# A convolution branch re-cut into a table of slots, with the order on three engines held as traced

## The chip, the cores and the metric

The program runs on one core of a Trainium2 chip. The metric is the device time of one execution in microseconds (us). Work is done by TensorE (PE in the profile; its weight loads are PEld), VectorE (DVE), ScalarE (ACT) and GpSimd (POOL). SyncE (SP) and, in the output stage, ScalarE's queue issue the DMA transfers.

## The reference

The function computed is a layer norm followed by two branches that are summed with the input, and then its whole backward pass: the value and the nine gradients are the outputs. B_x is an input that is not used.

```python
def _A_ref(q, k, v, shift_k, ssm_k, ssm_D):      # convolution branch
    k_shift = sum over 4 taps of k shifted by t * shift_k
    kv = k_shift * v
    y = irfft(rfft(kv padded to 2S) * rfft(ssm_k padded to 2S))[:S]
    y = y + kv * ssm_D
    return q * y

def _B_ref(x, W_gate, W_up, W_down):             # MLP branch
    gate = relu(x @ W_gate); up = x @ W_up
    return (gate * up) @ W_down

xn = _layernorm(A_q)
out = A_q + _A_ref(xn, A_k, A_v, A_shift_k, A_ssm_k, A_ssm_D) + _B_ref(xn, B_W_gate, B_W_up, B_W_down)
outputs: out and its gradients for A_q, A_k, A_v, A_shift_k, A_ssm_k, A_ssm_D, W_gate, W_up, W_down, given grad_out
```

The functions are condensed here. S is 2048, D is 1024, F is 3584, and everything is bf16.

## The kernel before

Two generators are interleaved while the program is traced. One, `mlp()` (L1028), yields the steps of the MLP: `hidden` (L699, gate, up and the gradient of the hidden layer, 8 matmuls of 128x512 a step), `grad_down` (L815) and `grad_in` (L850, weight gradients, also 8 matmuls a step). There are 336, 112 and 224 steps, and each yields 1730, meant as ns. In `hidden`, for each block of 512 columns and each pair of row tiles, the steps are two of gate (`ps_g`, relu by ScalarE, L726), two of up (`ps_u`, two VectorE operations, L733 and L735) and two of down (`ps_h`, a ScalarE copy L748 and a VectorE product L749). The first block, called ahead in the code, orders them differently, since it runs beside the layer norm.

The other generator is the convolution branch, `ABranch.steps` (L425). It treats the 1024 channels in 8 groups of 128. The transforms are two-stage DFTs by small matmuls against tables: `fwd1_filter` and `fwd1` (first stage), a transposition on VectorE (`flip`, L304, two operations of 1024 elements each), `fwd2` (second stage), `cmul` (complex products, ten VectorE operations), `inv_a`, `flip` and `inv_b` or `inv_b_chan` (inverse). ScalarE evicts the PSUM of all of them (L70). `taps` is the four-tap shift (seven VectorE operations, L74), `gate_grad` multiplies the gradient by xn, `grad_taps` and `grad_k` make the gradients of the shift, `loads_1` and `loads_2` load a group's data, and `h_tile` transposes the filter.

The main loop (L1033 to L1045) keeps a balance: each MLP step takes its ns times a pace (0.9 in `hidden`, 1.0 after it) from `left`, which begins at 55,000, and whenever `left` is at or under zero, the branch goes on to its next yield, which adds the ns it names. When the branch ends, its pools close and `open_right` (L868) issues the four loads of `wd`, the down weights of the output stage. Then come `out_phase` (L880 to L913), which needs `wd`, the transposed `hT` and three row tiles a step, and `grad_x`.

The traced order isn't the order on the engines. A scheduler places each instruction by its priority [...]. `Pri.now` (L31) gives the next priority in trace order; `Pri.late` (L35) puts it behind all of these, so that the branch's VectorE and ScalarE operations and its stores fill gaps. An instruction given to `keep_in_program_order` stays in its traced place. Before, that holds for a few: the first group's loads (L84), `shift_rows` (L227), the first sums and one product of the layer norm, and loads of the output stage.

Buffers matter too: the branch has two PSUM tiles (`a_ps`) and the MLP four (`b_ps`); `a_ts` has three buffers that kvt, gkv, gv, gks, yt, gk, hT and ghn share, so that a new one waits until the store of an old one has landed; `a_tmp` has two. Once the branch has closed, `wd` and `hT` take the space of its tiles.

Of the kernel before, what the change touches and what calls it, by code (L numbers as in the profile page):

```python
# [21 lines left out]
class Pri:  # L22
# [4 lines left out]
    def __init__(self, tc):  # L27
        self.tc = tc
        self.n = 0

# [12 lines left out]
class ABranch:  # L43
# [20 lines left out]
    def mm(self, out, lhsT, rhs, start=True, stop=True):  # L64
        self.pri.now()
        self.nc.tensor.matmul(out, lhsT=lhsT, rhs=rhs, start=start, stop=stop)  # L66

    def act(self, out, in_):
        self.pri.late()
        self.nc.scalar.copy(out=out, in_=in_)  # L70

    def tt(self, out, in0, in1, op):
        self.pri.late()
        self.nc.vector.tensor_tensor(out=out, in0=in0, in1=in1, op=op)  # L74

    def vcopy(self, out, in_):
        self.pri.late()
        self.nc.vector.tensor_copy(out=out, in_=in_)
# [11 lines left out]
    def open(self):  # L90
# [7 lines left out]
        self.tmp = self.pool("a_tmp", 2, side=R)  # L98
        self.sm = self.pool("a_sm", 2, side=R)
# [146 lines left out]
    def loads_1(self, gi):  # L246
# [5 lines left out]
        xt = self.tmp.tile([P, 16, P], BF16, name="xt", tag="tmp")  # L252
# [24 lines left out]
    def taps(self, st, out, src, offs):  # L277

        skb = st["skb"]
        for n, (i, off) in enumerate(offs):  # L280
            t = out if n == 0 else self.tmp.tile([P, 16, P], BF16, name="tap", tag="tmp")
            self.tt(t[:, 0:16, :], src[:, off:off + 16, :], skb[:, i, :, :].to_broadcast([P, 16, P]), ALU.mult)
            if n > 0:
                self.tt(out[:, 0:16, :], out[:, 0:16, :], t[:, 0:16, :], ALU.add)

    def h_tile(self, st):
# [4 lines left out]
        for r in range(16):  # L291
            self.pri.now()
            self.nc.tensor.transpose(pst[:, r, :], hv[:, r, :], self.identA[:])
# [3 lines left out]
    def flip(self, src):  # L297

        dst = self.big.tile([P, NB1, P], BF16, name="flp", tag="big")
        df = dst[:].rearrange("p k c -> p (k c)").bitcast(F32).rearrange("p (k cp) -> p cp k", cp=64)  # L300
        sf = src.rearrange("p cp r i -> p (cp r i)").bitcast(F32).rearrange("p (cp r) -> p cp r", cp=64)
        for c0 in range(0, 64, 32):
            self.pri.late()
            self.nc.vector.transpose(out=df[:, c0:c0 + 32, :], in_=sf[:, c0:c0 + 32, :])  # L304
        return dst

    def fwd1_filter(self, hT, sD, ns):
        B = self.big.tile([P, 64, NB1, 2], BF16, name="B", tag="big")
        for r0 in range(0, NB1, 8):
# [6 lines left out]
            if r0 == 0:  # L316
                for rows in (slice(0, 32), slice(64, 96)):
                    b0 = B[rows, :, 0, :]
                    self.tt(b0, b0, sD[rows].rearrange("p (cp i) -> p cp i", i=2), ALU.add)
            if r0 == 24:  # L320
                self.flipped = self.flip(B[:])
            yield ns

    def fwd1(self, src, ns):
        B = self.big.tile([P, 64, 2, 16, 2], BF16, name="B", tag="big")
        for r0 in range(0, 16, 8):
# [7 lines left out]
            if r0 == 8:  # L334
                self.flipped = self.flip(B[:].rearrange("p cp u r i -> p cp (u r) i"))
            yield 2 * ns

    def fwd2(self, Bf, F, ns):
        for j0 in range(0, 4, 2):
# [10 lines left out]
            yield 2 * ns  # L350
# [4 lines left out]
    def cmul(self, X, Z, conj, name):  # L355

        Q = self.form(name)
        for hf in range(2):
# [3 lines left out]
            self.tt(t1[:], X[:, g], Z[:, g], ALU.mult)  # L362
            self.tt(t2[:, 0], X[:, g, 0], Z[:, g, 1], ALU.mult)
            self.tt(t2[:, 1], X[:, g, 1], Z[:, g, 0], ALU.mult)
            self.tt(Q[:, g, 0], t1[:, :, 0], t1[:, :, 1], ALU.add if conj else ALU.subtract)
            self.tt(Q[:, g, 1], t2[:, 0], t2[:, 1], ALU.subtract if conj else ALU.add)
        return Q

    def inv_a(self, Q, ns):
        C = self.big.tile([P, 64, 4, 8, 2], BF16, name="C", tag="big")  # L370
        for j0 in range(0, 4, 2):
# [13 lines left out]
            if j0 == 2:  # L385
                self.flipped = self.flip(C[:].rearrange("p cp q m i -> p cp (q m) i"))
            yield 2 * ns

    def inv_b(self, Cf, dst, ns):
# [8 lines left out]
        yield 2 * ns  # L398

    def inv_b_chan(self, Cf, dst, ns):  # L400
        dv = dst[:, 0:16, :].rearrange("p r c -> p (r c)").rearrange("p (n1 n2) -> p n1 n2", n2=NB1)
        for n0 in range(0, NB1, 16):
# [4 lines left out]
            yield ns  # L407

    def grad_taps(self, gi, gks, kp, ns):


        ps = self.ps.tile([P, 2, 512], F32, name="ps6", tag="aps")
        self.mm(ps[:, 1, 0:3 * P], self.NX[:], gks[:, 0:3, :].rearrange("p r c -> p (r c)"))
        self.act(gks[:, 16:19, :].rearrange("p r c -> p (r c)"), ps[:, 1, 0:3 * P])
        pd = ps[:, 0, 0:P].rearrange("p (i c) -> p i c", i=4)
        for r in range(16):
            for b in range(0, P, 32):
                self.mm(pd[b:b + 32], gks[:, r, b:b + 32], kp[:, r:r + 4, b:b + 32], start=(r == 0), stop=(r == 15))
        dg = self.tmp.tile([P, 4, 32], F32, name="dg", tag="tmp")
        self.tt(dg[:], pd, self.ident32[:].to_broadcast([P, 4, 32]), ALU.mult)  # L420
        self.pri.late()
        self.nc.vector.tensor_reduce(out=self.gs_all[:, gi, :], in_=dg[:], axis=AX.X, op=ALU.add)
        yield ns

    def steps(self):  # L425

# [6 lines left out]
        yield 8000  # L433
        hT = self.h_tile(nx)
        for gi in range(self.NG):
            st, nx = nx, None
            cg, kp, vt, gt = st["cg"], st["kp"], st["vt"], st["gt"]
            yield 2000
            yield from self.fwd1_filter(hT, st["sD"], 2000)
            Hf = self.flipped  # L440
            if gi == 0:
                self.gate_grad(st)
            ksh = self.lng.tile([P, 16, P], BF16, name="ksh")
            self.taps(st, ksh, kp, [(3, 0), (2, 1), (1, 2), (0, 3)])
            kvt = self.ttile("kvt")
            self.tt(kvt[:, 0:16, :], ksh[:], vt[:], ALU.mult)
            yield from self.fwd1(gt, 2000)
            Gf = self.flipped
            H = self.form("H")
            yield from self.fwd2(Hf, H, 1700)  # L450
            if gi + 1 < self.NG:
                nx = self.loads_1(gi + 1)
            yield from self.fwd1(kvt, 1800)
            Kf = self.flipped
            G = self.form("G")
            yield from self.fwd2(Gf, G, 1700)
            if nx is not None:
                self.gate_grad(nx)
            GKV = self.cmul(H, G, True, "GKV")
            yield 2000  # L460
            K = self.form("K")
            yield from self.fwd2(Kf, K, 1700)
            Y = self.cmul(H, K, False, "Y")
            yield 12000
            yield from self.inv_a(GKV, 1800)
            Cg = self.flipped
            yield 5000
            yield from self.inv_a(Y, 1800)
            Cy = self.flipped
            GH = self.cmul(K, G, True, "GH")  # L470
            yield 2000
            gkv = self.ttile("gkv")
            yield from self.inv_b(Cg, gkv, 2000)
            gks = self.gradients(st, gkv, ksh)
            yield 6000
            yt = self.ttile("yt")
            yield from self.inv_b(Cy, yt, 2000)
            self.store_time(self.y_d, cg, yt)
            yield from self.grad_taps(gi, gks, kp, 1800)
            self.grad_k(st, gks)  # L480
            if nx is not None:
# [597 lines left out]
```

## Time and profile before

| what | value |
|---|---|
| median of 3 runs | 1955.04 us (1952.65 to 1960.59) |
| profiled execution, own time | 1959.32 us |
| its span | 1957.5 us |
| TensorE busy | 1898.6 us, 97% |
| VectorE busy | 904.3 us, 46% |
| ScalarE busy | 630.7 us, 32% |
| granted TensorE clock, mean | 0.994 |
| DMA | 319.08 MB, mean 163 GB/s |

The profile is of one execution. A busy time is the sum over an engine's instructions, and idle time is given with what ended it: "[3.72 <-DVE ru L733]" behind an instruction means that its engine stood 3.72 us and that the VectorE instruction of line 733 ended this. Idle time on an engine other than the one that sets the end costs nothing by itself. In the windows the columns are the window and its length, busy us and number of instructions of PE, PEld, DVE, ACT and POOL, the granted TensorE clock as a share of full speed, the busy share of the DMA engines and the GB/s that they moved.

By stage, the branch runs beside the MLP from about 99 to 1281 us; the MLP alone goes on to 1369; the output stage ends at 1562 and the last stage at 1957.

### The profile page before, as it was taken

The numbers are of one execution on the slowest core, as the hardware profiler recorded it, in microseconds if no ns is written. First come the engines' busy times: TensorE is split into PE (matmuls) and PEld (weight loads), VectorE is DVE, ScalarE is ACT, GpSimd is POOL, SyncE is SP. The second block draws the span as 40 slices with busy tenths as digits, with TensorE's granted clock in tenths as the row PEclk, the third lists the DMA queues.
The fourth block names the chain that finished last, engine by engine and source line by source line (L and its number), as shares of the span: only waits on it lengthen the run. The fifth ranks groups of instructions, "written<-read, shape, count | busy, mean of one in ns | idle before, by whom it ended". The sixth has DMA issues, their size and how long they took to land.

```text
span 1957.5 us, 35931 instructions
## 1 busy us (share of the span) xinstructions
PE 1898.6 (97%) x15291; PEld 884.2 (45%) x15530; DVE 904.3 (46%) x1348; ACT 630.7 (32%) x860; POOL 15.4 (1%) x38
## 2 busy tenths in 40 slices
PE   7989999999999999999999999999999999999998
PEld 3434444444444444444444444444444444444443
DVE  5768577578577655356255345300222222222222
ACT  5644444445445345344344444411000000000000
POOL 1000000000000000000000000000000000000000
PEclk9999999999999999999999999999999999999999
DMA  8885687875675684363663542592999954554451
GB/s 232 239 179 158 167 195 174 205 198 134 164 196 141 185 224 142 101 186 105 202 163 120 122 140 88 140 287 92 242 250 240 207 135 122 123 120 123 123 123 37
DMA packets 615969, 319.08 MB, mean 163 GB/s; under 512 B 450936, under 2 KB 585088, under 8 KB 615808
## 3 DMA queue, kind: packets, MB, share of 16 engines
q1 hardware_dynamic: 605312, 295.79, 60.2%
q10 hardware_dynamic: 9216, 16.78, 2.7%
q0 software_dynamic: 1280, 4.20, 0.6%
q8 instruction: 121, 1.98, 0.4%
q14 instruction: 40, 0.33, 0.1%
HBM read 141.56 MB, written 95.44 MB: 121 GB/s over the span
## 4 chain that ended last, share of the span: by engine, by line
PE 90%; issue 3%; DMA 3%; DVE 2%; ACT 1%; SPq 0%; POOL 0%; DVEq 0%; ACTq 0%; POOLq 0%
PE ps_w L810 20%; PE ps_x L944 18%; PE ps_o L910 10%; PE ps_g L662 9%; PE ps_d L810 9%; PE ps_u L662 9%; PE ps_h L662 9%; PE ps L66 6%; ACT ln_j L601 1%; DMA out_dram<-gv 1%; DMA ln_x<-in_A_q_dram 1%; DMA kp<-in_A_k_dram 1%; DVE ksh L74 0%; DMA ugs<-ug_d 0%; SPq L82 0%
## 5 line engine op out<-in xcount | busy, mean ns | idle before, releaser
L810 PE MATMUL ps_w<-ugs,xn_nat 128*128 128x512 bf16 x1730 | 393.0, 381 | 7.1 <-issue 4.0
L662 PEld LDWEIGHTS <-xnT 128*128 128x128 bf16 x1792 | 171.4, 98 | 228.0 <-issue 19.2
L810 PEld LDWEIGHTS <-xn_nat 128*128 128x128 bf16 x1792 | 171.3, 98 | 209.6 <-issue 8.2
L662 PE MATMUL ps_g<-wg,xnT 128*128 128x512 bf16 x866 | 208.0, 386 | 17.1 <-DVE xnT L688 11.3
L662 PE MATMUL ps_u<-wu,xnT 128*128 128x512 bf16 x864 | 201.6, 379 | 5.0 <-issue 2.3
L662 PE MATMUL ps_h<-wdT,goT 128*128 128x512 bf16 x869 | 202.0, 379 | 3.3 <-issue 2.1
L957 ACT ACTIVATE w<-xn,m 128x512 f32<-128x512 bf16 x32 | 24.3, 806 | 559.5 <-issue 317.2
L944 PE MATMUL ps_x<-wuT,guT 128*128 128x512 bf16 x879 | 197.6, 379 | 0.9
L944 PE MATMUL ps_x<-wgT,ggT 128*128 128x512 bf16 x877 | 197.3, 379 | 0.9
L910 PE MATMUL ps_o<-wd,hT 128*128 128x512 bf16 x878 | 192.6, 379 | 0.9
L810 PE MATMUL ps_d<-g_nat,hs 128*128 128x512 bf16 x801 | 183.3, 381 | 3.7 <-issue 3.1
L304 DVE STREAM_TRANSPOSE flp<-C 128x1024 f32<-128x1024 f32 x48 | 90.8, 1937 | 107.9 <-ACT C L70 107.9
L865 ACT CAST wi<-ps_w 128x512 bf16<-128x512 f32 x112 | 65.5, 585 | 223.7 <-PE ps_w L810 208.3
L944 PEld LDWEIGHTS <-ggT 128*128 128x128 bf16 x896 | 87.7, 98 | 105.7
L944 PEld LDWEIGHTS <-guT 128*128 128x128 bf16 x896 | 87.7, 98 | 105.7
L910 PEld LDWEIGHTS <-hT 128*128 128x128 bf16 x896 | 87.7, 98 | 105.7
L304 DVE STREAM_TRANSPOSE flp<-B 128x1024 f32<-128x1024 f32 x48 | 90.7, 1942 | 94.5 <-ACT B L70 94.5
L662 PEld LDWEIGHTS <-goT 128*128 128x128 bf16 x896 | 85.4, 98 | 104.2 <-issue 4.4
L810 PEld LDWEIGHTS <-hs 128*128 128x128 bf16 x832 | 79.1, 98 | 96.9 <-issue 5.6
L946 DVE CUSTOM_DVE_ANT_0 gx<-ps_x,gy 128x512 f32<-128x512 f32 x32 | 22.1, 692 | 214.4 <-PE ps_x L944 210.5
L733 DVE SCALAR_TENSOR_TENSOR ru<-ru,ps_u 128x512 bf16<-128x512 bf16 x112 | 76.5, 683 | 87.3 <-PE ps_u L662 49.4
L748 ACT CAST gh<-ps_h 128x512 bf16<-128x512 f32 x112 | 65.1, 584 | 157.8 <-PE ps_h L662 156.0
(166 smaller groups left out, 1487.9 us busy)
## 6 DMA issues: line engine op xcount, KB each, us to landing
ug_d<-ru SPq DMA_DIRECT2D x112, 256.0 KB, 2.9
ugs<-ug_d SPq DMA_DIRECT2D x112, 256.0 KB, 4.5
wg<-in_B_W_gate_dram SPq DMA_DIRECT2D x56, 256.0 KB, 4.1
wu<-in_B_W_up_dram SPq DMA_DIRECT2D x56, 256.0 KB, 4.3
h_d<-ht SPq DMA_DIRECT2D x112, 128.0 KB, 2.4
hs<-h_d SPq DMA_DIRECT2D x56, 256.0 KB, 4.6
out_dram<-wi SPq DMA_DIRECT2D x56, 256.0 KB, 3.3
gt<-in_grad_out_dram SPq DMA_DIRECT2D x32, 256.0 KB, 3.2
```

The lines of the kernel that those rows point to most:

```text
L66: self.nc.tensor.matmul(out, lhsT=lhsT, rhs=rhs, start=start, stop=stop)
L304: self.nc.vector.transpose(out=df[:, c0:c0 + 32, :], in_=sf[:, c0:c0 + 32, :])
L601: self.ln_act = nc.scalar.activation(out=jk[:, 0:cut], in_=xt[:, j, 0:cut], func=func, accum_out=sm[:, k, j:j + 1])
L662: self.nc.tensor.matmul(ps[:], lhsT=xT[:, kt * P:(kt + 1) * P], rhs=w(kt), start=(kt == 0), stop=(kt == self.DT - 1))
L733: nc.vector.scalar_tensor_tensor(out=ru[s][:, 1, :], in0=ru[s][:, 0, :], scalar=0.0, in1=ps[:], op0=ALU.is_gt, op1=ALU.mult)
L748: nc.scalar.copy(out=gh[:], in_=ps[:])
L810: self.nc.tensor.matmul(ps[:], lhsT=lhsT(st), rhs=rhs(st), start=(st == 0), stop=(st == self.ST - 1))
L865: nc.scalar.copy(out=wo[:, d, :], in_=ps[:])
L910: nc.tensor.matmul(ps[:], lhsT=hT[:, kt, :], rhs=self.wd[:, kt, oc], start=(kt == 0), stop=(kt == self.FT - 1))
L944: nc.tensor.matmul(ps[:], lhsT=T[:, kt, :], rhs=W[:, kt, oc], start=(i == 0), stop=(i == n - 1))
L946: V.tensor_tensor_reduce(out=gx[:, oc], in0=ps[:], in1=gy[:, oc], scale=1.0, scalar=0.0, op0=ALU.add, op1=ALU.add, accum_out=m[:, ob:ob + 1])
L957: nc.scalar.activation(out=w[:, oc], in_=xn[:, oc], func=ACT.Identity, scale=m[:, 5:6], bias=m[:, 4:5])
```

## The change

The branch's order is written out as a table, `slots`. A row is a pair: a TensorE step (or loads, or a small function) and a VectorE step, either of which may be None. The helpers `taps`, `flip` and `cmul` become generators that yield after every VectorE operation; the transforms yield after each TensorE step and no longer call `flip` themselves. `steps` runs one row and yields SLOT, 1900, for all of them. The table has 71 rows a group.

While the branch runs, `pri.strict` is set, from just before the first `h_tile` until the branch closes. In that time every matmul, every ScalarE eviction and every VectorE operation that both branches trace goes through `pin`, which keeps it in program order. DMA transfers are not pinned. The pace of `hidden` becomes 1.0. The tile xt gets a pool of its own (`a_xt`), the halo product of `grad_taps` a PSUM tile of its own, and in the layer norm the mean of chunk 2 is kept in order.

```diff
+    def pin(self, ins):
+        if self.strict:
+            self.tc.keep_in_program_order(ins)
...
     def mm(self, out, lhsT, rhs, start=True, stop=True):
         self.pri.now()
-        self.nc.tensor.matmul(out, lhsT=lhsT, rhs=rhs, start=start, stop=stop)
+        self.pri.pin(self.nc.tensor.matmul(out, lhsT=lhsT, rhs=rhs, start=start, stop=stop))
     def act(self, out, in_):
         self.pri.late()
-        self.nc.scalar.copy(out=out, in_=in_)
+        self.pri.pin(self.nc.scalar.copy(out=out, in_=in_))
     def tt(self, out, in0, in1, op):
         self.pri.late()
-        self.nc.vector.tensor_tensor(out=out, in0=in0, in1=in1, op=op)
+        self.pri.pin(self.nc.vector.tensor_tensor(out=out, in0=in0, in1=in1, op=op))
...
-        xt = self.tmp.tile([P, 16, P], BF16, name="xt", tag="tmp")
+        xt = self.xp.tile([P, 16, P], BF16, name="xt")
...
+    SLOT = 1900
...
         yield 8000
+        self.pri.strict = True
         hT = self.h_tile(nx)
+        yield 2000
         for gi in range(self.NG):
             st, nx = nx, None
...
+            for p, d in self.slots(st, hT, gi):
+                self.run(p)
+                self.run(d)
+                yield self.SLOT
+            nx, hT = st.get("nx"), st.get("hT_next")
         self.small_outputs()
...
+    def slots(self, st, hT, gi):
...
+        ksh = st["ksh"] = self.lng.tile([P, 16, P], BF16, name="ksh")
+        tk = self.taps(st, ksh, kp, [(3, 0), (2, 1), (1, 2), (0, 3)])
+        f1h = self.fwd1_filter(st, hT)
+        f1g = self.fwd1(st, "Bg", gt)
+        yield f1h, (lambda: self.gate_grad(st)) if gi == 0 else None
+        yield f1h, tk
+        yield f1h, self.both(lambda: self.add_D(st), tk)
+        yield f1h, tk
+        yield None, tk
+        flH = self.flip(st, "fH", st["Bh"][:])
+        yield f1g, flH
+        yield None, flH
+        yield f1g, tk
+        yield next_1, tk
+        f2H = self.fwd2(st, "H", "fH")
+        yield f2H, tk
+        flG = self.flip(st, "fG", st["Bg"][:].rearrange("p cp u r i -> p cp (u r) i"))
+        yield None, flG
+        yield f2H, flG
+        yield None, start_kvt
+        f2G = self.fwd2(st, "G", "fG")
+        yield f2G, None
+        yield None, None
+        yield f2G, None
+        f1k = self.fwd1(st, "Bk", st["kvt"])
+        yield f1k, None
+        q = self.cmul(st, "H", "G", True, "GKV")
+        yield None, q
+        yield f1k, q
+        yield None, q
+        yield None, q
+        flK = self.flip(st, "fK", st["Bk"][:].rearrange("p cp u r i -> p cp (u r) i"))
+        yield None, flK
+        yield None, flK
+        yield None, q
+        f2K = self.fwd2(st, "K", "fK")
+        yield f2K, q
+        yield None, q
+        yield f2K, q
+        yield None, q
+        iaG = self.inv_a(st, "Cg", "GKV")
+        yield iaG, q
+        qy = self.cmul(st, "H", "K", False, "Y")
+        yield next_gate, qy
+        yield iaG, qy
+        yield None, qy
+        yield None, qy
+        flg = self.flip(st, "fCg", st["Cg"][:].rearrange("p cp q m i -> p cp (q m) i"))
+        yield None, flg
+        yield None, flg
+        yield None, qy
+        iaY = self.inv_a(st, "Cy", "Y")
+        yield iaY, qy
+        yield None, qy
+        yield self.inv_b(st, "gkv", "fCg"), qy
+        yield None, qy
+        yield None, start_gv
+        yield None, qy
+        yield None, start_gks
+        qh = self.cmul(st, "K", "G", True, "GH")
+        yield iaY, qh
+        yield None, qh
+        yield lambda: self.halo(st), qh
+        yield None, qh
+        yield lambda: self.tap_sums(st), None
+        yield None, lambda: self.tap_diagonals(st)
+        fly = self.flip(st, "fCy", st["Cy"][:].rearrange("p cp q m i -> p cp (q m) i"))
+        yield next_2, fly
+        yield None, fly
+        yield None, qh
+        iaH = self.inv_a(st, "Ch", "GH")
+        yield iaH, qh
+        yield None, qh
+        yield self.both(self.inv_b(st, "yt", "fCy"), store_y), qh
+        yield None, qh
+        yield None, qh
         gk = self.ttile("gk")
-        self.taps(st, gk, gks, [(0, 0), (1, 1), (2, 2), (3, 3)])
+        tg = self.taps(st, gk, st["gks"], [(0, 0), (1, 1), (2, 2), (3, 3)])
+        yield None, tg
+        yield iaH, tg
+        yield None, tg
+        yield None, tg
+        flh = self.flip(st, "fCh", st["Ch"][:].rearrange("p cp q m i -> p cp (q m) i"))
+        yield None, flh
+        yield None, flh
+        yield None, tg
+        yield None, tg
+        yield None, tg
         self.store_time(self.out_gk, st["cg"], gk)
+        yield next_h, None
+        ib = self.inv_b_chan(st, "fCh")
+        yield ib, None
+        yield None, None
+        yield ib, None
+        yield None, lambda: self.store_gh(st)
...
-            average(0, b(0))
+            mean = average(0, b(0))
+            if i == 2:
+                self.tc.keep_in_program_order(mean)
...
-        yield 0.9, b.hidden(first, goT, load, ln, a.tables, B_W_gate, B_W_up, B_W_down, g, xn_d, h_d, ug_d)
+        yield 1.0, b.hidden(first, goT, load, ln, a.tables, B_W_gate, B_W_up, B_W_down, g, xn_d, h_d, ug_d)
...
                     if d is None:
                         a.close()
                         a_steps = None
+                        pri.strict = False
                         b.open_right(B_W_down)
```

The small functions in the table do what stood between the yields before: `next_1`, `next_2`, `next_gate` and `next_h` are `loads_1`, `loads_2`, `gate_grad` and `h_tile` of the next group; `start_kvt`, `start_gv` and `start_gks` are single VectorE products; `halo`, `tap_sums` and `tap_diagonals` are the former `grad_taps`; `store_gh` and `store_y` issue stores.

## The prediction, made before the changed kernel was run

> **What bounds the kernel now.** First the page's busy line and the slices by stage, to see which engine leaves no room:
>
> ```profile
> PE 1898.6 (97%) x15291; PEld 884.2 (45%) x15530; DVE 904.3 (46%) x1348; ACT 630.7 (32%) x860; POOL 15.4 (1%) x38
> ```
> TensorE is busy for 1898.6 of 1957.5 us, so 58.9 us are all that any new order can win, and whatever makes TensorE wait is paid in full. The windows by stage place these: 14.9 us idle before 100 us (start-up), 18.5 us in 100 to 694, 9.0 in 694 to 950, 5.8 in 950 to 1369, 0.9 in the output stage, 9.3 in the last stage, of which the last slice alone has 7.7. The change can reach the middle three, about 33 us. TensorE's wait list and the timeline name the large ones:
>
> ```profile
> 120.28 0.42 PE L66 MATMUL ps<-flp,FW 64*32 64x128 bf16 x32 [1.05 <-ACT B L70]
> ...
> 134.94 5.18 PE L662 MATMUL ps_g<-wg,xnT 128*128 128x512 bf16 x16 [3.72 <-DVE ru L733]
> ```
> ```profile
> 253.31 0.63 PE L66 MATMUL ps<-RB,flp 128*128 128x64 bf16 x16 [1.68 <-ACT hT L70]
> ```
> ```profile
> 387.72 1.23 DVE L74 TENSOR_TENSOR gk<-gks,skb 128x2048 bf16<-128x2048 bf16 x1 [4.21 <-DMA out_dram<-gv]
> ...
> 389.20 0.72 PE L66 MATMUL ps<-GH,IA 32*64 32x128 bf16 x60 [2.02 <-DVE dg L74]
> ```
> ```profile
> 718.33 1.23 DVE L74 TENSOR_TENSOR gk<-gks,skb 128x2048 bf16<-128x2048 bf16 x1 [12.86 <-DMA out_dram<-gv]
> ...
> 725.22 1.01 PE L66 MATMUL ps<-RB,flp 128*128 128x64 bf16 x16 [3.02 <-ACT hT L70]
> ```
> The reader sees one pattern: convolution work is traced in lumps, a lump's VectorE or ScalarE part is late (twice behind the store of gv, whose buffer gk takes), and TensorE's next small matmul waits. The line at 134.94 shows an after-effect: 16 matmuls in 5.18 us where 16 elsewhere take 3.62. The windows give the cause:
>
> ```profile
> 135.00:139.00 4.00, 4.00 (x12) 1.46 (x12) 2.57 (x5) 0.57 (x1) 0.00 (x0) 0.61 0.58 134
> ```
> The granted clock (third figure from the end) is 0.61; it falls likewise after the stalls at 389 and 725 (0.66 and 0.57), not after the one of 1.68. So a stall of 2 us or more costs 1.6 us besides.
>
> Last the hand-over to the output stage, from SP's timeline:
>
> ```profile
> 1276.10 0.38 SPq L875 DMA_DIRECT2D wd<-in_B_W_down_dram  x1
> ...
> 1281.26 4.98 SPq L880 DMA_TRANSPOSE hT<-h_d  x1
> ...
> 1291.23 6.85 SPq L880 DMA_TRANSPOSE hT<-h_d  x1
> ...
> 1298.76 4.16 SPq L880 DMA_TRANSPOSE hT<-h_d  x1
> 1303.01 0.82 SPq L88 DMA_DIRECT2D out_dram<-so  x2
> 1303.88 0.41 SPq L875 DMA_DIRECT2D wd<-in_B_W_down_dram  x1
> ...
> 1319.73 0.37 SPq L875 DMA_DIRECT2D wd<-in_B_W_down_dram  x1
> ```
> The output stage starts at 1369.2. Its weights wd (4 loads of 1.8 MB) can start only when the convolution branch has closed, and land here by about 1332, 37 us early. Before, this lead costs nothing.
>
> [...] VectorE stood 12.86 us at one gk with other work behind it. [...] In 1307 to 1327, while wd arrived, the windows show 359 to 397 GB/s moved (reads and other transfers together).
>
> **The change part by part.**
>
> *Slots in place of lumps.* A channel group has 71 slots of 1900 ns of the MLP's time, 134.9 us, where the yields of before summed to 119. No operation goes or comes: the same 15,300 matmuls and 1348 VectorE operations, only gks's halo has a PSUM tile of its own. Each slot has one VectorE operation of 0.69 (cmul), 1.22 (taps) or 1.94 us (flip) against 1.9 us of MLP time, plus the MLP's own VectorE load in the hidden stage, 0.683+0.422+0.686 = 1.79 per three steps of 1.73. VectorE has for a group 12 flips x 1.94 + 18 x 1.22 + 6 x 1.22 + 24 x 0.69 + 1 = 70 us and the MLP's 134.9/5.19 x 1.79 = 47, 117 in some 151 us (134.9 and about 16 of small matmuls on TensorE). It fits. gk is now 17 slots behind gv's store, hT is four slots ahead of its use, gate_grad has an xt of its own. So I let the four stalls go: 1.05+3x0.50+3.72+1.6 = 7.8 in the first group, 1.7, 2.0+1.6 = 3.6, 3.0+1.6 = 4.6. Sum 17.7 us gained. Late next is the start-up, costed below. The wait for xn_nat at 930 and the 1.7 us at 71 lie outside the table; I leave them.
>
> *The held order.* TensorE's step in slot n is traced behind VectorE's operation of slot n-1. Most steps come two slots or more behind what they read. Two come one slot behind: the first inv_a step of Y (slot 37, reads the sum of slot 36) and of GH (slot 53, sum of slot 52), each after two flips. A group is 134.9 us, just under 78 steps of the MLP, and 78 is 13 rounds of gate, gate, up, up, down, down; so all four groups in the hidden stage meet the same phase. For GH: end of a gate step at 0, first flip done by 0.9; the up step ends at 1.73, its two VectorE operations at 2.83; second flip to 4.77; the next up's two to 5.88; the sum to 6.57 (about 6.4 with the overlap of some 0.06 us that the timeline shows between neighbours). TensorE gets there at 3 x 1.73 = 5.18. Stall 1.2 us, four times: +4.8. For Y there is a spare step and nothing is lost. Behind a waiting VectorE operation stand the MLP's evictions; its four PSUM banks cover four steps, 6.9 us.
>
> *An earlier start.* The pace of the hidden stage goes from 0.9 to 1.0, so the first loads are traced after step 32 instead of 36, and slot 1 comes at step 38. Nothing speeds the loads: SP issued hn at 94.0 and ended skb's issue at 110.1, and skb takes 4.2 us to land, 20 us after hn began. sk_d, which skb reads, needs sk_t from ScalarE, which ran the tables until 91.5. I take hn at 89 (bounds 86 and 93). Then kp and skb are there at 109, while VectorE reaches the first tap (slot 2) at about 97.5. It stands 11 us; the up step behind it gets its eviction at 109+1.22+0.68 = 111; TensorE runs out of banks at 105.6. Stall 5.4, clock 1.6, and the lag that is left at fwd2 of H and G some 2.5: +9.5 us (bounds 3 and 16, by the same sum from 86 and 93). It eats what the first group gained.
>
> *The end of the branch.* MLP time is 672 steps x 1730 = 1162.6 us. Before, the branch takes 55/0.9 for its start and ends 51 steps ahead of the end (88 us in the trace: 1281 to 1369). After, 55+8+2+568x1.9 = 1144.2: it closes at step 662, 10 steps or 17.3 us ahead. The wd loads inherit the late priority of the last store in small_outputs (open_right sets none), so hT's three transposes go first, as above. From the branch's last matmul: three transposes hold SP 4.98+6.85+4.16 = 16 us, then so, then three wd loads of 5.5 MB, 15 us at 370 GB/s and 18 at 300. All landed about 18 us after the MLP ends; the first chunk is there sooner. The first tile needs 28 matmuls of 0.216, the last seven of them the last chunk: 18+1.5 against 6.0, stall 13.5; with clock 1.6 and something for ya, xe and xr on the same engines, +16 us. Bounds: 3 where all four go ahead of the transposes, 30 where a chunk falls behind the three wgT transposes (14 us at 1374).
>
> *Sum.* -17.7 + 4.8 + 9.5 + 16 = +12.6 us. On the profiled execution (span 1957.5, 1.8 around it, 1959.3) that is 1971.9; it lies 4.3 above the median 1955.0 of the runs, and to the median it gives 1967.6.
>
> **Rivals.**
> A: wd is hidden anyway. If wd 2 to 4 are put right behind the first, before the transposes, they land within the 17 us, and 16 falls to about 1: -2.4, 1952.6, not slower. It decides once the last chunk lands less than 4 us after the MLP's end. For it: SP has no slabs (ugs) to issue by then; against: that three of the four waited behind hT before.
> B: as A, and the first group's loads are early too (hn at 86 or earlier, 9.5 becomes 2): -10, 1945. Against: the tables on ScalarE until 91.5.
> C: the held order makes VectorE wait for DMA landings in many groups, since stores still have low priority on SP while everything behind stands: 2 to 4 us a group over 8 groups, 16 to 32 more: 1992. For it: gk's waits for gv, 23.1 us in four; against: 17 slots between them now.
> D: the change does less than it says, the stalls of before remaining by other causes: 17.7 halves, 1976.
>
> **How the numbers follow.** Forecast 0.40 (1967.6, own range 1959 to 1977), A 0.23, B 0.12, C 0.13, D 0.12. Range 1946 to 1986: it holds the forecast, A, D, half of B and the lower part of C. About 0.5% (9.8 us) is what can be told from no change. Faster: B and the best of A, 0.16. Within: most of A and the low third of the forecast, 0.28. Slower: 0.56.
>
> **What would show it.** Right: idle TensorE of 10 us or more where ps_o starts, ended by wd, with a clock near 0.6 after it; a stall near 105 us ended by a VectorE eviction, VectorE waiting for kp or skb; four stalls of about 1.2 us before GH's inv_a ended by VectorE; no wait for hT or dg. Wrong: wd landed before the first ps_o (A), or VectorE's waits for DMA spread over the groups (C).

## The result, and the profile after

The changed kernel takes 1974.57 us (median of 4 runs, 1973.49 to 1975.30) beside 1956.56 us for the kernel before (4 runs): the ratio is 1.0091, with a 95% interval of 1.0069 to 1.0114. The profiled execution took 1973.85 us with a span of 1972.1, 14.6 more than the span of before.

The page after, first its busy line, then two of its costliest groups (line, operation and tiles, busy us and mean ns, and the idle time ahead of them with what ended it):

```profile
PE 1921.9 (97%) x15530; PEld 883.7 (45%) x15530; DVE 906.3 (46%) x1348; ACT 629.7 (32%) x860; POOL 15.5 (1%) x38
...
L925 PE MATMUL ps_w<-ugs,xn_nat 128*128 128x512 bf16 x1792 | 403.8, 381 | 5.3 <-DMA xn_nat<-xn_d 4.9
...
L1026 PE MATMUL ps_o<-wd,hT 128*128 128x512 bf16 x896 | 197.6, 384 | 14.2 <-DMA wd<-in_B_W_down_dram 14.2
```
VectorE is as busy as before. TensorE shows 23.3 us more busy time, which is no new work: in the trace of before 239 matmul records are missing (15291 against 15530 weight loads), and matmuls at half clock (0.50 granted, at 135 to 138 us before and at 121 to 127 after) last longer (up to 0.63 us each in both traces, beside 0.38). So here the busy sum is a poor measure, and the marks of the stages tell more. They are ends and starts of groups of matmuls in the two traces, in us:

| mark | before | after | after less before |
|---|---|---|---|
| last transposition of the layer norm (pst_x) | 51.9 | 45.2 | -6.7 |
| end of `hidden` (last ps_h) | 700.6 | 696.0 | -4.6 |
| end of `grad_down` | 929.0 | 918.2 | -10.8 |
| end of `grad_in` (last ps_w) | 1369.4 | 1365.6 | -3.8 |
| end of the output stage (last ps_o) | 1562.8 | 1577.3 | +14.5 |
| end | 1957.5 | 1972.1 | +14.6 |

The changed kernel is ahead until the MLP ends and loses 18.3 us in the output stage. There the page of before has next to no idle time:

```profile
L910 PE MATMUL ps_o<-wd,hT 128*128 128x512 bf16 x878 | 192.6, 379 | 0.9
```
TensorE's waits after, summed by what ended them (total us, times, longest):

```profile
PE ps_o L1026 <- DMA wd<-in_B_W_down_dram: 14.2, 2, 9.7
PE ps_g L776 <- DVE xnT L802: 6.2, 4, 2.9
PE ps_u L776 <- DMA wu<-in_B_W_up_dram: 5.0, 2, 4.6
PE ps_w L925 <- DMA xn_nat<-xn_d: 4.9, 7, 2.3
PE ps L72 <- DVE GH L80: 4.3, 4, 1.1
PE ps_g L776 <- DVE ru L847: 3.2, 2, 2.3
```
The stalls of before are gone: hT's 4.7 us have become 0.3, and the waits for dg and for B are no longer in the list. Five others stand in their place. The hand-over first, in SP's timeline after (start, duration, issued transfer, number of issues):

```profile
1348.30 7.24 SPq L996 DMA_TRANSPOSE hT<-h_d  x2
...
1356.20 4.02 SPq L996 DMA_TRANSPOSE hT<-h_d  x1
...
1361.19 0.41 SPq L991 DMA_DIRECT2D wd<-in_B_W_down_dram  x1
...
1362.26 0.46 SPq L991 DMA_DIRECT2D wd<-in_B_W_down_dram  x1
...
1366.66 0.84 SPq L991 DMA_DIRECT2D wd<-in_B_W_down_dram  x1
1377.84 13.81 SPq L1018 DMA_TRANSPOSE wgT<-in_B_W_gate_dram  x3
1391.70 0.57 SPq L991 DMA_DIRECT2D wd<-in_B_W_down_dram  x1
```
and in TensorE's timeline after (the bracket holds the idle time before the group):

```profile
1370.04 19.97 PE L1026 MATMUL ps_o<-wd,hT 128*128 128x512 bf16 x84 [4.45 <-DMA wd<-in_B_W_down_dram]
1399.73 25.44 PE L1026 MATMUL ps_o<-wd,hT 128*128 128x512 bf16 x107 [9.72 <-DMA wd<-in_B_W_down_dram]
```
All four loads of wd stand behind three transposes of hT, and the fourth behind three more, of wgT. The 84 matmuls are four tiles of 21: all that three of the four chunks allow. Then TensorE stands until the last chunk, issued at 1391.70, is there. The windows after show what follows from it and from two other stalls (columns as in front; the third figure from the end is the granted clock):

```profile
120.00:128.00 8.00, 5.80 (x14) 1.84 (x14) 3.03 (x4) 0.00 (x0) 0.00 (x0) 0.57 1.04 234
...
922.00:934.00 12.00, 8.14 (x19) 1.97 (x19) 7.32 (x9) 0.58 (x1) 0.00 (x0) 0.57 1.02 331
1369.00:1374.00 5.00, 3.96 (x11) 1.50 (x12) 0.62 (x1) 0.00 (x0) 0.00 (x0) 0.66 1.05 400
...
1400.00:1405.00 5.00, 5.00 (x15) 1.83 (x14) 0.69 (x1) 0.00 (x0) 0.00 (x0) 0.58 0.00 0
```
At full clock (1.00 granted) a matmul of this shape comes every 0.216 us: 16 in a row take 3.62 us in both traces, the last of them 0.38. So the 84 need 18.1 us and took 19.97, and the next 107 need 23.1 and took 25.44. Waits and half clock together: 4.45 + 9.72 + 1.8 + 2.3 = 18.3 us, the 18.3 of the table.

### The profile page after: what moved, and what is told of

It is laid out like the page before. It is cut to its first block, busy times and chain, and to the rows that moved or that the text cites. A ratio compares the mean times of both kernels' runs of the same rounds, so it can differ in the third digit from the quotient of the medians.

```text
span 1972.1 us, 36183 instructions
## 1 busy us (share of the span) xinstructions
PE 1921.9 (97%) x15530; PEld 883.7 (45%) x15530; DVE 906.3 (46%) x1348; ACT 629.7 (32%) x860; POOL 15.5 (1%) x38
## 4 chain that ended last, share of the span: by engine, by line
PE 89%; DMA 3%; DVE 3%; issue 2%; SPq 2%; ACT 1%; DVEq 0%; ACTq 0%
PE ps_w L925 20%; PE ps_x L1060 19%; PE ps_d L925 9%; PE ps_o L1026 9%; PE ps_g L776 9%; PE ps_u L776 8%; PE ps_h L776 8%; PE ps L72 6%; SPq L88 1%; DMA ln_x<-in_A_q_dram 1%; PE ps_d L946 1%; SPq L1018 1%; ACT ln_j L713 1%; DMA out_dram<-wi 1%; DVE flp L313 1%
## 5 line engine op out<-in xcount | busy, mean ns | idle before, releaser
L925 PE MATMUL ps_w<-ugs,xn_nat 128*128 128x512 bf16 x1792 | 403.8, 381 | 5.3 <-DMA xn_nat<-xn_d 4.9
L925 PEld LDWEIGHTS <-xn_nat 128*128 128x128 bf16 x1792 | 170.9, 98 | 216.6 <-DMA xn_nat<-xn_d 11.3
L776 PE MATMUL ps_u<-wu,xnT 128*128 128x512 bf16 x896 | 208.0, 382 | 6.7 <-DMA wu<-in_B_W_up_dram 5.0
L1026 PE MATMUL ps_o<-wd,hT 128*128 128x512 bf16 x896 | 197.6, 384 | 14.2 <-DMA wd<-in_B_W_down_dram 14.2
L76 ACT CAST B<-ps 128x1024 bf16<-128x1024 f32 x96 | 94.0, 1015 | 78.1 <-PE ps L72 72.7
```

Of the source, the lines that this page charges most:

```text
L76: self.pri.pin(self.nc.scalar.copy(out=out, in_=in_))
L776: self.pri.pin(self.nc.tensor.matmul(ps[:], lhsT=xT[:, kt * P:(kt + 1) * P], rhs=w(kt), start=(kt == 0), stop=(kt == self.DT - 1)))
L925: self.pri.pin(self.nc.tensor.matmul(ps[:], lhsT=lhsT(st), rhs=rhs(st), start=(st == 0), stop=(st == self.ST - 1)))
L1026: nc.tensor.matmul(ps[:], lhsT=hT[:, kt, :], rhs=self.wd[:, kt, oc], start=(kt == 0), stop=(kt == self.FT - 1))
```

## The experiments

The kernel before was run beside every experiment, and its medians lay between 1956.06 and 1956.95, so the experiments can be set beside one another to about a us.

**e1_before_mean.** The mean of chunk 2 alone, on the kernel before.

```diff
-            average(0, b(0))
+            mean = average(0, b(0))
+            if i == 2:
+                self.tc.keep_in_program_order(mean)
```


> The kernel before with only the held mean of chunk 2 in the layer norm (the one edit of the change that acts ahead of the branch). In the two traces the changed kernel reaches step 32 of the MLP 6.8 us earlier. Theory: this one edit makes the 6.8 us; then ps_sk, the small transpose of the shift taps, comes at 84 instead of 90.6 us and the time is about 1950 (-6 to -7). Rival: the start differs by how the layer norm's inputs happen to land in one execution, or through the placement of other work; then the time stays at 1955 to 1958.

1950.50 us (8 runs), ratio 0.9964 (0.9953 to 0.9976). In its trace the last pst_x ends at 47.2 instead of 51.9, and TensorE's waits for xnT sum to 7.4 instead of 11.3. VectorE's timelines show the way: before, the mean of chunk 2 (at 12.37) and the work behind it ran ahead of the copy that gives TensorE its first xnT, which came at 18.23; with the mean held the copy goes first, at 10.97 in the timeline of the changed kernel, and in this run TensorE's longest wait for xnT is 3.4 us instead of 9.1. So one part of the change, which the prediction didn't price, gains 6.5 us.

**e2_wd_now.** The loads of wd at once, on the changed kernel.

```diff
+        self.pri.now()
         for a in range(0, self.FT, 7):
             self.nc.sync.dma_start(out=self.wd[:, a:a + 7, :],
```


> The changed kernel with one line more: wd's loads get the current priority in place of the late one, so that all four stand ahead of the second hT transpose on SP. Theory (the late end of the branch costs through the order of wd behind the transposes): the two waits for wd, 4.45 and 9.72 us, and most of the slow clock after them go; 1974.6 becomes 1957 to 1962. Rival (the 17 us that are left hold too little time for 7.3 MB whatever the order, or hT's transposes become late in turn): waits of 8 us or more stay at the first ps_o, ended by wd or hT, and the time is 1968 or more.

1967.12 us (8 runs, 1963.41 to 1975.22), ratio 1.0053 (1.0036 to 1.0069), between the two theories. SP's timeline of this run shows why:

```profile
1347.46 3.61 SPq L997 DMA_TRANSPOSE hT<-h_d  x1
1351.24 9.39 SPq L992 DMA_DIRECT2D wd<-in_B_W_down_dram  x4
1360.74 9.20 SPq L982 DMA_DIRECT2D out_dram<-wi  x3
1369.99 20.15 SPq L997 DMA_TRANSPOSE hT<-h_d  x3
```
and its TensorE waits:

```profile
PE ps_o L1027 <- DMA hT<-h_d: 3.8, 2, 2.3
PE ps_o L1027 <- DMA wd<-in_B_W_down_dram: 2.8, 2, 1.5
```
The four loads are issued by 1360.6, but the transposes of hT that stood ahead of them are now behind, and hT is late instead. So the order on SP is worth 7.5 us, but this order, the only other one that was tried, did not take all of the wait away: what goes behind comes after its use.

**e4_slot1840.** The slots shorter, on the changed kernel, so that the branch closes 568 x 0.060 = 34 us earlier in traced time.

```diff
-    SLOT = 1900
+    SLOT = 1840
```


> The changed kernel with a slot of 1840 ns instead of 1900: the branch ends 568 x 0.06 = 34 us of MLP time earlier, 51 us ahead of the output stage. Theory (the end of the branch sets the loss): both waits for wd go, and with them the slow clock, -18 us; the shorter slots bring VectorE nearer its limit in the hidden stage and break the fixed phase, which gives back 0 to 4: 1956 to 1961. Rival (the held order is the loss, and tighter slots make it worse): stalls ended by VectorE grow in all four groups of the hidden stage, and the time stays above 1967.

1964.44 us (9 runs), ratio 1.0035 (1.0025 to 1.0045): 10 us gained, not 18. No wait for wd is left, and the output stage takes 193.4 us, as before the change. But the hidden stage ends at 706.7 instead of 696.0. VectorE's timeline of this run:

```profile
387.45 1.23 DVE L80 TENSOR_TENSOR gk<-gks,skb 128x2048 bf16<-128x2048 bf16 x1 [12.65 <-DMA out_dram<-gv]
```
SP's:

```profile
382.96 1.07 SPq L94 DMA_DIRECT2D out_dram<-gv  x1
```
and TensorE's:

```profile
391.72 6.01 PE L776 MATMUL ps_g<-wg,xnT 128*128 128x512 bf16 x16 [7.12 <-DVE ru L847]
```
The old wait of gk for the store of gv is back. The last part of that store was issued at 382.96, and the MLP's evictions, which come behind gk in VectorE's held order, waited with it (the next ru is at 390.99, the last one before it at 374.10). The wait of 7.12 us and the half clock after it (0.53 granted in 391 to 397 us; 16 matmuls in 6.01 us, where 3.62 suffice) make 9.5 us at this one place. This is the rival in which the held order makes VectorE wait for a transfer, in one group.

**e9_slot1840_store_now.** As e4_slot1840, with the stores no longer late: `store` calls `pri.now()`.

```diff
-        self.pri.late()
+        self.pri.now()
```


> The kernel with slots of 1840 and one line more: the branch's stores get the current priority instead of the late one. In the run with 1840 alone VectorE stood 12.65 us at gk for the store of gv, which SP issued some 40 us after it was traced, and TensorE 7.1 us with half clock after it. Theory (low-priority stores against a held order make that stall): it goes, 1964.4 becomes 1953 to 1957. Rival (SP is full there, stores in front delay the loads that TensorE needs): waits for wu, wg, wdT or kp of 4 us or more come in its place, and the time stays above 1961.

1960.36 us (11 runs), ratio 1.0021 (1.0011 to 1.0031). The stores of this gv are issued by 341.4 and the stall of 7.1 is gone, but only 4.1 us are gained, between the two theories: a wait of 2.7 for goT is new. That these stores now stand ahead of the MLP's loads on SP would explain it; it wasn't tested apart.

**e5_before_late_end.** A late end alone, on the kernel before: pace 1.0, and a balance that makes the branch end as late as after the change.

```diff
-        yield 0.9, b.hidden(first, goT, load, ln, a.tables, B_W_gate, B_W_up, B_W_down, g, xn_d, h_d, ug_d)
+        yield 1.0, b.hidden(first, goT, load, ln, a.tables, B_W_gate, B_W_up, B_W_down, g, xn_d, h_d, ug_d)
...
-                        left += d
+                        left += d * 1.134
```


> The kernel before, its lumps and its free order kept, with the pace of the hidden stage at 1.0 and every yield of the branch longer by 1.134, so that the branch closes at step 662 of the MLP as in the changed kernel. Theory (the late end alone makes the loss at the output stage): waits for wd of 10 us or more at the first ps_o and slow clock after them, +15 to +21 on 1957, some of the stalls of the lumps easier: 1968 to 1977. Rival (the free order places wd's loads in time whatever the end, the loss comes from the held order): no wait for wd above 3 us and 1957 or less.

1961.01 us (12 runs), ratio 1.0013 (1.0001 to 1.0025). That is less than the theory expected. The output stage takes 201.5 us, 8.1 more than before. SP's timeline of this run:

```profile
1341.96 0.38 SPq L875 DMA_DIRECT2D wd<-in_B_W_down_dram  x1
...
1346.02 0.47 SPq L875 DMA_DIRECT2D wd<-in_B_W_down_dram  x1
...
1353.41 7.90 SPq L880 DMA_TRANSPOSE hT<-h_d  x2
...
1367.93 0.54 SPq L875 DMA_DIRECT2D wd<-in_B_W_down_dram  x1
1378.32 15.30 SPq L902 DMA_TRANSPOSE wgT<-in_B_W_gate_dram  x3
```
Two loads go ahead of hT here and the other two (the third at 1366.84) ahead of wgT; one wait of 5.21 us for wd remains, as TensorE's waits show:

```profile
PE ps_o L910 <- DMA wd<-in_B_W_down_dram: 5.2, 1, 5.2
...
PE ps L66 <- ACT hT L70: 2.2, 1, 2.2
PE ps L66 <- ACT ghn L70: 2.0, 1, 2.0
...
PE ps_g L662 <- DVE ru L733: 1.2, 2, 0.9
```
So a late end costs 8 us with this order on SP and 18 with that of the changed kernel: the lateness is one cause, the place of the loads behind the transposes the other.

The total grew by 4.6 us only, since the stages ahead of it became shorter. The lumps are all still there, and yet the waits for B and dg are gone, the longest for ru is 0.9 us instead of 3.7, and of hT's two one is left; one for ghn is new. From the last pst_x to the end of `grad_down` this run takes 867.6 us, the kernel before 877.1 and the changed kernel 873.0.

**e7_gap16.** A later start of the branch, on the changed kernel, 8 us of MLP time more between the first loads and the first slot, and slots of 1886 (568 x 0.014 = 8.0 us), so that the branch still ends at the same place.

```diff
-    SLOT = 1900
+    SLOT = 1886
...
-        yield 8000
+        yield 16000
```


> The changed kernel with 8 us of MLP time more between the first group's loads and its first step, and slots of 1886 in place of 1900, so that the branch ends where it did. Theory (the first group starts before xt, kp and skb have landed, VectorE stands and takes TensorE with it): the stall of 2.3 us near 100 goes, the wait for wu near 117 (4.6 us) shrinks to 1 or less since its loads stood on SP behind stores of late VectorE results, with their slow clock: -6 to -10, 1965 to 1968. Rival (wu's loads are late for a reason of their own, the buffers or the next group's loads ahead of them): a wait of 3 us or more for wu stays, -2 to -4, 1970 to 1973.

1959.61 us (12 runs), ratio 1.0010 (1.0001 to 1.0019): 15.0 us gained, more than expected. Its waits of TensorE:

```profile
PE ps_o L1026 <- DMA wd<-in_B_W_down_dram: 14.2, 2, 9.9
...
PE ps_w L925 <- DMA xn_nat<-xn_d: 3.2, 7, 0.9
...
PE ps L72 <- DVE GH L80: 1.1, 3, 0.8
```
The waits for wd are untouched. Those of the first group (wu and ru) are gone, and `hidden` ends at 681.8 instead of 696.0. GH's have fallen from 4.3 to 1.1, which is 3 of the 15; probably slots of 1886 meet the MLP's steps differently, but that wasn't tested apart.

**e3_gh_later.** GH's step one slot later, on the changed kernel.

```diff
-        yield iaH, qh
         yield None, qh
+        yield iaH, qh
```


> The changed kernel with the first inv_a step of GH one slot later, two slots behind the sum that it reads. Theory (held order: TensorE comes 1.1 us before VectorE's sum in the four groups of the hidden stage): the four waits of 1.08 to 1.09 us on GH go, -4.3 us, 1970.3. Rival (TensorE's wait only moves to another place, the flips' lag being the cause): they turn up at the next step that follows, and the time stays within 1 us of 1974.6.

1970.84 us (4 runs), ratio 1.0069 (1.0049 to 1.0090): 3.7 us gained and no wait for GH left, as the theory had it.

**e6_free.** No held order at all, on the changed kernel.

```diff
-        self.pri.strict = True
```


> The changed kernel, its table of slots and all else kept, with nothing held in order (strict is never set). Theory (the order costs only the four waits on GH, 4.3 us, and part of the first group): those waits go, wd's stay, 1965 to 1971. Rival 1 (holding the order is what removed the old stalls, the table alone does not): stalls of 2 us or more ended by VectorE or ScalarE come back in the hidden stage and the time is 1975 or more. Rival 2 (the order costs much more, for example at xn_nat, 5 us and 10 us of half clock): below 1963.

1975.84 us (4 runs), ratio 1.0087 (1.0069 to 1.0105), no different from the changed kernel. GH's waits are gone, and grad_in takes 440.5 us instead of 447.4, but the first group stalls more: 6.1 and 2.8 us at flp, 1.6 at kvt. The waits for wd stay (8.8, and 4.7 that the trace puts down to a store). The old stalls at hT and dg do not come back, so it isn't the held order that removed them.

**e11_free_grad_in.** The held order ended at grad_in, on the changed kernel.

```diff
+        self.pri.strict = False
         xn = self.nat_tiles(xn_d, "xn_nat")
```


> The changed kernel with the order held only up to grad_in: strict is cleared there, so the last third of the branch is placed freely. Theory (held order keeps the small matmuls of the branch from filling TensorE's waits for xn_nat, which in the run without any held order were 0.8 us in place of 4.9, without the 10 us of half clock): the stretch from the end of grad_down to the end of grad_in gets 6 to 7 us shorter, 1966 to 1969. Rival (xn_nat's loads merely met other DMA traffic there): the waits stay and so does the time, 1973 to 1976.

1968.68 us (4 runs), ratio 1.0059 (1.0042 to 1.0076): 5.9 us gained. TensorE's timeline there, first of the changed kernel:

```profile
920.54 0.39 PE L925 MATMUL ps_w<-ugs,xn_nat 128*128 128x512 bf16 x1 [0.89 <-DMA xn_nat<-xn_d]
...
926.13 1.27 PE L925 MATMUL ps_w<-ugs,xn_nat 128*128 128x512 bf16 x2 [2.31 <-DMA xn_nat<-xn_d]
```
then of this one:

```profile
920.74 5.17 PE L925 MATMUL ps_w<-ugs,xn_nat 128*128 128x512 bf16 x21 [0.59 <-DMA xn_nat<-xn_d]
...
926.80 0.82 PE L925 MATMUL ps_w<-ugs,xn_nat 128*128 128x512 bf16 x3 [0.73 <-DMA xn_nat<-xn_d]
927.55 0.23 PE L72 MATMUL ps<-flp,FW 64*32 64x128 bf16 x3
927.72 0.82 PE L925 MATMUL ps_w<-ugs,xn_nat 128*128 128x512 bf16 x3
```
and ScalarE's of this one:

```profile
933.66 1.56 ACT L982 CAST wi<-ps_w 128x512 bf16<-128x512 f32 x3 [11.80 <-PE ps_w L925]
```
Without the held order TensorE does three large matmuls for each row tile of xn that arrives, with a few of the branch's small ones between them. Three results are then copied out back to back, so it worked on three output tiles at a time. With the held order it finishes one output tile before it begins the next, does one matmul for each row tile and stands, in view of work that it may not take. The rival, other DMA traffic, does not explain it: in both traces SP issued eight row tiles from 915.0 (915.9) on and eight from 921.4 (922.3) on, and 333 GB/s were moved between 920 and 930 us.

**e8_split.** The parts together, on the changed kernel: the gap of 16000, GH one slot later, stores not late, and slots of 1780 from the fifth group on, which leaves the first four at 1900.

```diff
-                yield self.SLOT
+                yield self.SLOT if gi < 4 else 1780
```


> All that the runs so far point to, with the order held: the first step 8 us after the loads, GH's step one slot later, stores at the current priority, and slots of 1780 in the last four groups, where the MLP leaves VectorE free, so that the branch ends about 44 us ahead of the output stage. If the pieces add up (8 us of gap: -11 in the first group; GH -4.3; wd's waits and their half clock -18), 1974.6 becomes 1938 to 1945, below the kernel before with the held mean (1950.5). If they overlap, or DMA traffic moves a wait elsewhere, 1946 to 1955.

1950.76 us (5 runs), ratio 0.9968 (0.9955 to 0.9981). The parts do not add up to the 1938 to 1945 of the expectation: together, with the order held, they end where the kernel before ends with the held mean alone (1950.50). No wait for wd; new is one for hs, in TensorE's timeline of this run:

```profile
694.14 1.03 PE L946 MATMUL ps_d<-g_nat,hs 128*128 128x512 bf16 x2 [3.28 <-DMA hs<-h_d]
```
**e10_split_free.** As e8_split, and with the held order ended at grad_in (the edit of e11_free_grad_in).

> The same with the order held only up to grad_in. If the waits for xn_nat are the held order's, another 5 to 7 us less than the run beside it: 1932 to 1940. If not, the same time as that run within 2 us; if the free order brings the late VectorE steps back in the last groups, 2 to 5 us more than it.

1940.47 us (4 runs), ratio 0.9916 (0.9901 to 0.9931): 16.4 us under the kernel before, 34 under the changed one and 10 under the kernel before with the held mean alone. In the traces `grad_in` takes 439.2 us, beside 447.1 in e8_split, and the start-up is 1.8 us shorter. The wait for hs stays (4.0 us in three).

**e12_split_unheld.** As e10_split_free, but with no held order anywhere, that is without `self.pri.strict = True`.

> e10_split_free with the held order left out altogether (strict is never set); slots, gap, stores and the rest as there. Theory (holding the order of the engines is worth little either way, since e6_free moved the unchanged slots by 1.3 us only, and its losses stood in the first group where loads were late, which the longer gap has mended): 1935 to 1944 us, no stall of over 2 us ahead of 600 us. Rival 1 (the held order is what keeps VectorE's and ScalarE's late-priority operations from falling behind, and e10 gains by it): small matmuls of the branch wait for ScalarE or VectorE again, as the kernel before does at hT and dg, 1948 us or more. Rival 2 (without it the scheduler closes the branch at another time): the loads of wd change their place by over 10 us, and the output stage waits or not with them.

1940.84 us (4 runs), ratio 0.9910 (0.9891 to 0.9929). The wait for hs is gone; one of 3.9 us for flp is new. It stands at 117 us, where none of over 2 us was expected. Its line among TensorE's waits:

```profile
PE ps L72 <- DVE flp L313: 3.9, 1, 3.9
```
So once the loads are in time at both ends, holding the order up to `grad_in` changes nothing that these runs can measure. In `grad_in` it costs: between e8_split and e10_split_free lie 10.3 us, of which the traces place 7.9 there.

## Why the prediction came out as it did

**The sum.** Of the profiled execution the prediction was 1971.9, and it took 1973.85. To the median it was 1967.6 against 1974.57, inside the range. Of those 7.0 us, 4.3 are a shift that applied to one kernel only: the profiled execution of before lay above its median, that of after 0.7 below its own. How near the sum came is in good part luck: two terms that it lacks cancel, and one has the right size by another course, as below. And its bound of 58.9 us for all that an order can win was not one: 12.6 of this idle time have no cause in the profile, only "issue", of which the trace of after, with no record missing, lists none of note; and what half clock costs is busy time (up to 0.63 us for a matmul of 0.38).

**Slots in place of lumps, -17.7.** Right as to the stalls: all four are gone, with their spells of half clock (1.00 granted in 128 to 694 and in 694 to 915 after). That the table did it is not shown. In the run with a late end alone a group also takes 134.9 us of MLP time instead of 119, but keeps its lumps, and it gains 9.5 us over the same stretch. So about half of the term comes with the slower pace alone; how much the table adds to that wasn't measured.

**The held order, +4.8.** Right in place, number and size: four waits at GH of 1.08 to 1.09 us, 4.3 together, and 3.7 us back when the step is moved by one slot.

**The earlier start, +9.5.** The size was right by luck, for half of the course was wrong. VectorE did stand 11.0 us, but in two parts, in its timeline after:

```profile
92.09 1.23 DVE L80 TENSOR_TENSOR gt<-gt,xt 128x2048 bf16<-128x2048 bf16 x1 [5.44 <-DMA xt<-xn_d]
...
99.96 1.23 DVE L80 TENSOR_TENSOR ksh<-kp,skb 128x2048 bf16<-128x2048 bf16 x1 [5.59 <-DMA h_d<-ht]
```
and TensorE's says what it cost:

```profile
101.84 1.89 PE L776 MATMUL ps_g<-wg,xnT 128*128 128x512 bf16 x8 [2.30 <-DVE ru L847]
...
121.80 1.01 PE L776 MATMUL ps_u<-wu,xnT 128*128 128x512 bf16 x2 [4.64 <-DMA wu<-in_B_W_up_dram]
```
skb was issued at 93.8 and was there at about 100, not at 109. The loads took about as long as predicted, but hn, the first, was issued at 81.2 and not at 89, earlier than the bound of 86: the transposition ps_sk, which makes skb's source, ran at 77.0 instead of 90.6, by the shorter start-up (6.7 us) and by the pace (four steps of the MLP, 6.9 us). (The second VectorE wait is put down to a store; skb, issued 1.5 us before that store, is what the operation reads.) So the first stall was 2.3 us instead of 5.4 and left the clock alone (1.00 in 98 to 104). What the sum did not have is the next load behind: the four loads of wu were issued only at 117.96, after the stores of the late VectorE results and the next group's loads, and TensorE stood for them (4.64 + 0.39) and then ran 14 matmuls in 5.80 us where 3.02 suffice (clock 0.57 in 120 to 128). Together 2.3 + 5.0 + 2.8 = 10.1. That late loads are the cause is shown by the run with the longer gap. That SP's queue made wu late is read from the timeline.

**The end of the branch, +16.** The mechanism was right: the branch closes late, wd goes behind hT, TensorE waits and its clock falls (0.66 in 1369 to 1374, 0.58 in 1400 to 1405). The term is 18.3. The step that failed is the order of the chunks. "The first chunk is there sooner" was false: it went behind hT too, which gave the wait of 4.45. And the bound at which a chunk falls behind wgT, kept at 30 us, is what happened. It cost less than 30 because the scheduler ran three quarters of four tiles before it needed that chunk, where the prediction let the first tile wait.

**What the sum left out.** Two terms, which nearly cancel. "The change can reach the middle three" stages was wrong: it reached the start-up too, which ran 6.7 us shorter. The held mean was in the diff and got no price, though 14.9 us of idle time stood in the stretch that it touches. Alone it moves the last pst_x by 4.7 us; in the twelve traces that have it this mark lies at 45.0 to 47.2, in the two without it at 51.9 and 54.3, so the other 2 us are within the spread of single executions. And grad_in took 447.4 us instead of 440.4: the prediction left the wait for xn_nat out as "outside the table", but the held order reaches it, because it forbids TensorE other work in the gaps. In the kernel before, the branch's small matmuls ran there:

```profile
930.54 0.39 PE L810 MATMUL ps_w<-ugs,xn_nat 128*128 128x512 bf16 x1 [0.78 <-DMA xn_nat<-xn_d]
930.86 0.31 PE L66 MATMUL ps<-GKV,IA 32*64 32x128 bf16 x13
```
Priced in full: -6.7 - 17.7 + 4.3 + 10.1 + 7.0 + 18.3 = +15.3, against 14.6 measured. The -17.7 in it is the predicted figure, not a measured one; the 0.7 that remain are not assigned.

**The rivals.** A, wd hidden, did not occur, and so neither did B as a whole. But B's own half did: hn was issued before 86, and the first stall cost 2.3 us where B had put 2; the later wait for wu took back what this won. C, VectorE held at landings in many groups, did not occur either in the changed kernel, though its mechanism is real: it returned for 7.1 us when only SLOT was changed. D had the wrong cause, since the old stalls went in full; its 1976 was nearer to the measured time than the forecast, so the traces tell the two apart, not the time.

## What to carry to other kernels

Where one stream of work is re-timed against another, price its two ends first: which loads must land before its first step, which loads can only start after its last, and what stands ahead of them on the issuing queue. In the middle the stalls went as predicted, though about half of that gain came with a slower pace alone, and both ends together gave away 28 us. And the held order cost 5.9 us where loads arrived one by one, at `grad_in`: wherever a wait for data remains, ask what else the engine would have done in it.

## What the runs showed of the hardware

- The clock falls not only after one long stall. At 919 to 923 us after the change TensorE waited 0.89, 0.28, 0.29 and 0.27 us, with one matmul between each, and the clock was at half from 922.9 on (0.96 in 922 to 923, 0.50 in 923 to 926), before the wait of 2.31. The kernel before shows the same: after waits of 0.78, 0.51 and 0.36 us within 3 us the clock is 0.64 in 934 to 938. After waits of 1.49 and 1.34 us with five us of work between them (the run with wd at once) it stayed at full speed (1.00 in 1369 to 1382); the following one of 2.27 brought it down (0.72 in 1382 to 1388). And the wait of 2.30 us ahead of 101.84 after the change left it at 1.00 (98 to 104). So the prediction's 2 us for one stall is no limit in these traces; what makes the clock fall was not shown.
- After the change the half-speed spells (0.50 granted) lasted 3.4 us (from 1370), 6.8 (from 120.8) and 10.2, the longest ones where the matmuls went on waiting for transfers (922.9 to 933.2, and 1394 to 1404, of which TensorE idled 5.7).
- SP is held for long by transposing transfers: three of wgT took 13.81 us of issue after the change and 15.30 in the late-end run, three of hT 20.15 in the run with wd at once, against 0.37 to 0.84 for one plain load of wd of 1.8 MB in the traces of before and after, where they stood singly.
- One VectorE operation of 0.17 us, kept in its place, was worth 6.5 us at the start, as it no longer went ahead of the copy of xnT that TensorE's first step waits for (at 10.97 us after the change, at 18.23 before).
